# A grouped 1x1 convolution: one extra ring piece of 32 rows, moved by transfers that use 4 of the 16 DMA engines

## The chip, the cores and the metric

The kernel runs on one core of one Trainium2 chip. The metric is the device time of one execution in microseconds (us), and smaller is better. Each profile shows one execution.

The engines are named as the profile names them: PE is the matrix engine (PEld its weight loads), DVE the vector engine, ACT the scalar engine, SP the engine that issues the loads. ACTq and SPq are the queues of ACT and SP, where transfers are issued. Sixteen DMA engines carry the transfers: around 300 us the trace of the kernel before has 16.0 packets under way on average. "Packet" is one record of a transfer in the trace, read here as what one DMA engine moves at a time. A large piece of this kernel makes packets of 24,576 bytes, 128 for its load and 128 for its store. "Instruction fetch" is said here of the packets of 16,384 bytes on queue q8, a queue that the profile lists as "instruction" (12 packets in the kernel before).

## The reference

```python
def reference(x, w):              # x: (1, 512, 512, 192) bf16; w: (1, 1, 4, 48, 48) bf16
    xg = x.reshape(1, 512, 512, 4, 48)
    out = einsum('bhwgc,gcd->bhwgd', xg, w[0, 0])      # cut: the loops over a 1x1 window
    return out.reshape(1, 512, 512, 192)
```

Each of the 262,144 pixels has 192 channels in four groups of 48, and each group is multiplied by its own 48x48 matrix. 100.7 MB come in and 100.7 MB go out.

## The kernel before

Pixels are cut into "pieces". A piece of `size` columns puts `size` consecutive pixels into each of the 128 partitions. One column is thus 128 pixels, and the whole problem is 2048 columns. Loads go into a ring of 256 columns in `x_sb`; results go into a ring of the same size in `o_sb` and are stored from there, piece by piece. The compute engines work in groups of 4 columns: six transposes, a copy by DVE, six matmuls and an eviction from PSUM by ACT (every fourth group is shared with DVE). There are 512 groups.

```python
BIG = 64; RCOLS = 256
HEAD = (4, 4, 8, 16, 32); TAIL = (32, 16, 8, 4, 4)
LOOK = 3; ST_DELAY = 2
# ...
    sizes = list(head) ...                            # head, as many BIG as fit, the rest, tail
    for s in sizes + [BIG] * (mid // BIG) + ([mid % BIG] if mid % BIG else []) + last:
        whole = s == BIG and c % BIG == 0
        pieces.append(Piece(c, s, ("big", c // BIG % (RCOLS // BIG)) if whole else ("own", len(pieces))))
        c += s
# ...
    loads = plan_pieces(cols, HEAD, TAIL)
    stores = plan_pieces(cols, HEAD, TAIL)
    def rows_view(ap, p):                             # 128 rows: 16 landings in the trace
        return ap[128 * p.col:128 * (p.col + p.size), :].rearrange("(p i) c -> p (i c)", p=128)
# ...
        def wait_out_free(wq, g):                     # the ring's place must have been stored
            if g >= body:
                p = store_at[g - body]
                wq.wait(st_sem[p.key], st_val[p])
# ... SP:
            for p in loads:
                wq.wait(t_done, p.g1 - body)          # the ring's place must have been read by PE
                sp.dma_start(ring_view(x_sb, p), rows_view(xf, p)).then_inc(ld_sem[p.key], 16)
# ... ACT:
            def store(p):
                act.dma_start(rows_view(of, p), ring_view(o_sb, p)).then_inc(st_sem[p.key], 16)
            for g in range(NG):
                wait_out_free(wq, g)
                wq.wait(mm_done, g + 1)
                while pending and pending[0][1] <= g:
                    store(pending.pop(0)[0])
                # ... eviction of group g ...
                if g in store_end:                    # a piece is stored once its LAST group is out
                    pending.append((store_end[g], g + ST_DELAY))
```

A wait for a piece is over only when the slowest of the engines that carry it has landed its share: ACT's last wait for the ring, until 424.60 us, is for a store whose fifteenth landing came at 408.76 us and whose last came at 425.07 us (424.58 on the timeline's axis, see below).

Of the kernel before, what the change touches and what calls it, by code (L numbers as in the profile page):

```python
# [11 lines left out]
C = GROUPS * CG  # L12
# [12 lines left out]
BIG = 64  # L25
RCOLS = 256
HEAD = (4, 4, 8, 16, 32)
TAIL = (32, 16, 8, 4, 4)
# [2 lines left out]
LOOK = 3  # L31
ST_DELAY = 2
RING = 8


class Waiter:

    def __init__(self, eng):
        self.eng = eng
        self.seen = {}  # L40
# [7 lines left out]

class Piece:

    def __init__(self, col, size, key):
        self.col, self.size, self.key = col, size, key
        self.g0, self.g1 = col // 4, (col + size) // 4


def plan_pieces(cols, head, tail):
    sizes = list(head) if cols >= sum(head) + sum(tail) else []
    last = list(tail) if sizes else []
    mid = cols - sum(sizes) - sum(last)
    pieces, c = [], 0  # L60
    for s in sizes + [BIG] * (mid // BIG) + ([mid % BIG] if mid % BIG else []) + last:
        whole = s == BIG and c % BIG == 0
        pieces.append(Piece(c, s, ("big", c // BIG % (RCOLS // BIG)) if whole else ("own", len(pieces))))
        c += s
    return pieces


def bass_standalone__grouped__vision_kernel(nc, x, w, out):
    B, H, W_, Cx = x.shape
    assert Cx == C and tuple(w.shape) == (1, 1, GROUPS, CG, CG)  # L70
    npix = B * H * W_

    cols = npix // 128
    assert npix % 512 == 0, "the pixel count must be a multiple of 512"
    NG = cols // 4
    loads = plan_pieces(cols, HEAD, TAIL)
    stores = plan_pieces(cols, HEAD, TAIL)
    load_of = {p.g0: p for p in loads}
    store_at = {g: p for p in stores for g in range(p.g0, p.g1)}
    store_end = {p.g1 - 1: p for p in stores}  # L80
# [1 line left out]
    xf = x.rearrange("b h w c -> (b h w) c")  # L82
    of = out.rearrange("b h w c -> (b h w) c")
    wv = w.rearrange("a b g c d -> c (a b g) d")

    body = RCOLS // 4
    assert body % RING == 0 and BIG % 4 == 0 and RCOLS % BIG == 0
    bigs = [p for p in loads if p.key[0] == "big"]
# [4 lines left out]
    def shared(g):  # L93
        return g % 4 == 1 and g < NG - 3

    dve_prog = [("wcopy", 0)]
    for g in range(NG + LOOK):
        if g < NG:
# [2 lines left out]
        if 0 <= h < NG and shared(h):  # L101
            dve_prog.append(("ev2", h))

    def rows_view(ap, p):
        return ap[128 * p.col:128 * (p.col + p.size), :].rearrange("(p i) c -> p (i c)", p=128)

    def ring_view(t, p):
        at = p.col % RCOLS
        assert at + p.size <= RCOLS
        return t[:, at * C:(at + p.size) * C]  # L110

    with ExitStack() as es:
        block = es.enter_context(nc.Block())
        x_sb = es.enter_context(nc.sbuf_tensor("x_sb", [128, RCOLS * C], BF16))
        o_sb = es.enter_context(nc.sbuf_tensor("o_sb", [128, RCOLS * C], BF16))
# [11 lines left out]
        ld_sem = {k: sem(f"ld_{k[0]}{k[1]}") for k in dict.fromkeys(p.key for p in loads)}  # L127
        st_sem = {k: sem(f"st_{k[0]}{k[1]}") for k in dict.fromkeys(p.key for p in stores)}
        st_val, seen = {}, {}
        for p in stores:  # L130
            seen[p.key] = seen.get(p.key, 0) + 16
            st_val[p] = seen[p.key]
        w_sem, id_sem, e_sem, wb_sem, wc_sem = (sem(s) for s in ("w_sem", "id_sem", "e_sem", "wb_sem", "wc_sem"))
        p0_sem, p1_sem = sem("p0_sem"), sem("p1_sem")
        t_done, mm_done = sem("t_done"), sem("mm_done")
        e1_sem = [sem(f"e1_{i}") for i in range(RING)]
        fa_sem = [sem(f"fa_{i}") for i in range(RING)]
        d2_sem = [sem(f"d2_{i}") for i in range(2)]
# [19 lines left out]
        @block.sync  # L158
        def _(sp):
            wq = Waiter(sp)  # L160
            sp.dma_start(w_sb[:], wv).then_inc(w_sem, 16)  # L161
            for p in loads:
                wq.wait(t_done, p.g1 - body)
                sp.dma_start(ring_view(x_sb, p), rows_view(xf, p)).then_inc(ld_sem[p.key], 16)  # L164

        @block.tensor
        def _(pe):

            def build_weights():
                pe.wait_ge(e_sem, 1)  # L170
                pe.wait_ge(w_sem, 16)
                last = None
                for (tc, r, g, c0_) in WBLOCKS:
                    s0 = ESHIFT - r
                    col = WOFF[tc] + c0_
                    last = pe.matmul(o_ps[:, NOB - 1, col:col + CG], lhsT=esel[:, s0:s0 + 128],  # L176
                                     rhs=w_sb[:, g, :], start=True, stop=True, skip_group_check=True)
                last.then_inc(wb_sem, 1)

            def transposes(g):  # L180
                if g == 0:
                    pe.wait_ge(id_sem, 1)
                p = load_of.get(g)
                if p:
                    pe.wait_ge(ld_sem[p.key], 16)
                ins = []
                for ul in range(2):
                    u = g % body * 2 + ul
                    for tc in range(3):
                        col = u * UC + tc * 128  # L190
                        j = ul * 3 + tc
                        ins.append(pe.transpose(xT_ps[:, g % NXP, j * 128:(j + 1) * 128],  # L192
                                                x_sb[:, col:col + 128], ident[:]))
                if p:
                    ins[1].then_inc(ld_sem[p.key], -16)
                ins[-1].then_inc(t_done, 1)

            def matmuls(g):
                xs = xT_sb[g % NXP]
                waited = [e1_sem[g % RING]]  # L200
                if g == 0:
                    pe.wait_ge(wc_sem, 1)
                if g >= 2:
                    waited.append(fa_sem[(g - 2) % RING])
                    if shared(g - 2):
                        waited.append(d2_sem[(g - 2) // 4 % 2])
                for s in waited:
                    pe.wait_ge(s, 1)
                ins = []
                for ul in range(2):  # L210
                    v = 2 * g + ul
                    for tc in range(3):
                        j = ul * 3 + tc
                        c0_, c1_ = COLR[tc]
                        ins.append(pe.matmul(o_ps[:, v % NOB, c0_:c1_], lhsT=xs[:, j * 128:(j + 1) * 128],  # L215
                                             rhs=wt[:, WOFF[tc]:WOFF[tc] + (c1_ - c0_)],
                                             start=(tc == 0), stop=(tc == 2), skip_group_check=True))
                for i, s in enumerate(waited):
                    ins[1 + i].then_inc(s, -1)
                ins[-1].then_inc(mm_done, 1)  # L220

            def step(g):
                if g + LOOK < NG:
                    transposes(g + LOOK)
                matmuls(g)

            build_weights()
            for g in range(min(LOOK, NG)):
                transposes(g)
            for g in range(loop_g0 if reps else 0):  # L230
                step(g)
            if reps:
                with pe.Fori(0, reps, 1):
                    for g in range(loop_g0, loop_g0 + body):
                        step(g)
            for g in range(loop_g1 if reps else 0, NG):
                step(g)

        @block.vector
        def _(dve):  # L240
            wq = Waiter(dve)
            for (op, g) in dve_prog:
# [4 lines left out]
                if op == "ev1":  # L247
                    wq.wait(t_done, g + 1)
                    dve.tensor_copy(xT_sb[g % NXP][:], xT_ps[:, g % NXP, 0:2 * UC]).then_inc(e1_sem[g % RING], 1)  # L249
                else:  # L250
# [7 lines left out]
        @block.scalar  # L258
        def _(act):
            wq = Waiter(act)  # L260
            pending = []

            def store(p):
                act.dma_start(rows_view(of, p), ring_view(o_sb, p)).then_inc(st_sem[p.key], 16)  # L264

            for g in range(NG):
                wait_out_free(wq, g)
# [3 lines that stand above are left out]
                v = 2 * g  # L271
                u = g % body * 2
                if shared(g):
                    ins = act.copy(o_sb[:, u * UC:(u + 1) * UC], o_ps[:, v % NOB, 0:UC])  # L274
                else:
                    dst = o_sb[:, u * UC:(u + 2) * UC].rearrange("p (u c) -> p u c", u=2)
                    ins = act.copy(dst, o_ps[:, v % NOB:v % NOB + 2, 0:UC])  # L277
                ins.then_inc(fa_sem[g % RING], 1)
                if g in store_end:
                    pending.append((store_end[g], g + ST_DELAY))  # L280
            for (p, _) in pending:
                act.wait_ge(fa_sem[(p.g1 - 1) % RING], 1)
                store(p)
            for p in stores:
                if st_val[p] == seen[p.key]:
                    wq.wait(st_sem[p.key], st_val[p])
# [28 lines left out]
```

## Time and profile before

| | before |
|---|---|
| time, median of 3 runs | 492.08 us (491.52 to 492.30) |
| span of the profiled execution | 489.8 us |
| PE busy | 423.4 us (86%) |
| DMA moved | 201.63 MB, mean 412 GB/s |

From the profile's page of the kernel before: its line of busy times (share of the span, instructions), two lines of its 40 equal slices of the span (DMA is the mean busy share of the 16 DMA engines in tenths, GB/s what they moved), and the two lines of the chain of waits that ended last, by engine and by line.

```profile
PE 423.4 (86%) x6154; PEld 407.9 (83%) x6154; DVE 336.1 (69%) x640; ACT 357.2 (73%) x513; POOL 1.3 (0%) x8
...
DMA  8999999999999999999999999999999999998593
GB/s 297 430 425 423 428 430 433 427 435 425 436 425 432 433 431 433 429 432 431 425 433 430 429 435 429 434 429 433 429 429 426 438 421 434 421 424 351 238 385 149
...
DMA 77%; PE 18%; ACT 1%; another core or an unknown queue 1%; issue 1%; SPq 1%; ACTq 0%
DMA out_dram<-o_sb 73%; PE o_ps L215 10%; PE xT_ps L192 8%; DMA x_sb<-in_x_dram 4%; ACT o_sb L277 1%; SPq L164 0%; ACTq L264 0%; SPq L161 0%; ACTq L46 0%
```

The transfers are the limit: the DMA engines are at 9 tenths in nearly all slices, at about 430 GB/s, and 73% of the chain is stores. But slices 37 to 40 break off. This is the view by stretches for the last 32 us.

```profile
core 0: us, PE busy (x) PEld busy (x) DVE busy (x) ACT busy (x) POOL busy (x), PEclk, DMA share, GB/s
458.00:466.00 8.00, 6.92 (x107) 6.58 (x105) 5.80 (x12) 5.87 (x10) 0.00 (x0) 1.00 0.30 123
466.00:474.00 8.00, 7.32 (x113) 6.95 (x110) 6.36 (x13) 7.33 (x11) 0.00 (x0) 1.00 0.99 416
474.00:482.00 8.00, 3.84 (x30) 3.11 (x30) 0.56 (x1) 2.45 (x4) 0.00 (x0) 0.79 0.64 264
482.00:490.00 8.00, 0.00 (x0) 0.00 (x0) 0.00 (x0) 0.80 (x1) 0.00 (x0) 0.62 0.35 133
```

In two of these stretches the DMA engines are on average only a third busy. An average of 0.30 can be sixteen engines at a third or a few engines at full time. The records of the trace decide: each transfer of 128 rows leaves sixteen landings, read here as one for each engine that carried it. Landings and packet times stand in this document on a clock on which the last landing falls on the end of the span. On the axis of the timelines they are 0.5 us earlier (the last landing of the kernel before is at 489.35 us there). Distances between landings are the same on both; a distance from an instruction to a landing is 0.5 us shorter than the numbers here make it. Of the sixteen landings of one store, the fifteenth and the last are these (us).

```
store of one large piece    15th      last      gap
1st lap of the ring         76.54     76.62     0.1
3rd                        192.98    197.49     4.5
5th                        309.65    318.89     9.2
7th                        424.24    437.96    13.7
final store                485.54    489.84     4.3
```

One engine falls behind by about 2 us a lap. Its store packets take 0.985 to 1.0 us, the others' 0.912. At the end it is the only engine that works: around 463 us and from 486 to 489 us the mean number of busy engines in the trace is 1.0. For the last load PE stands and waits, as the waits of the stretch 440 to 490 us show (engine, line, what it waited for: total us, times, longest us).

```profile
PEld xT_ps L192 <- DMA x_sb<-in_x_dram: 4.1, 1, 4.1
PE xT_ps L192 <- DMA x_sb<-in_x_dram: 3.9, 1, 3.9
```

The timeline of ACT (start in us, duration, instruction, idle time before it and what ended that) gives the last wait for a place in the ring and the last eviction.

```profile
424.60 0.80 ACT L277 CAST o_sb<-o_ps 128x768 bf16<-128x768 f32 x1 [2.76 <-DMA out_dram<-o_sb]
...
482.02 0.80 ACT L277 CAST o_sb<-o_ps 128x768 bf16<-128x768 f32 x1 [0.43 <-PE o_ps L215]
```

The last eviction ends at 482.8 us, fifteen engines have landed everything at 485.5 us, and the span ends with the slow engine at 489.8 us. The last 4.3 us belong to that engine alone.

### The profile page before, as it was taken

How to read it: one execution, taken by the hardware profiler on the slowest of the kernel's cores; microseconds unless marked ns; L12 is line 12 of the kernel's file. 1: busy time of each engine (PE TensorE's matmuls, PEld its weight loads, DVE VectorE, ACT ScalarE, POOL GpSimd, SP SyncE). 2: the span in 40 equal slices, each digit the busy share in tenths (PEclk: the TensorE clock that was granted, in tenths of full speed). 3: DMA queues.
4: the chain of work that ended last, by engine and by line, in shares of the span. 5: the costliest groups of instructions: out<-in, count | busy, mean ns of one | idle time of the engine just before them, and what ended most of it. 6: DMA issues, size and time to landing. Idle time of an engine off the chain costs nothing.

```text
span 489.8 us, 14171 instructions
## 1 busy us (share of the span) xinstructions
PE 423.4 (86%) x6154; PEld 407.9 (83%) x6154; DVE 336.1 (69%) x640; ACT 357.2 (73%) x513; POOL 1.3 (0%) x8
## 2 busy tenths in 40 slices
PE   5999989977997979979798979899798979799962
PEld 5899989977987879878788878898787978799862
DVE  3688878867675767757676757767577757588750
ACT  2788878866785767767677757678586868688862
POOL 1000000000000000000000000000000000000000
PEclk9999999999898998989998989989899989899996
DMA  8999999999999999999999999999999999998593
GB/s 297 430 425 423 428 430 433 427 435 425 436 425 432 433 431 433 429 432 431 425 433 430 429 435 429 434 429 433 429 429 426 438 421 434 421 424 351 238 385 149
DMA packets 11750, 201.63 MB, mean 412 GB/s; under 512 B 1488, under 2 KB 2512, under 8 KB 3536
## 3 DMA queue, kind: packets, MB, share of 16 engines
q1 hardware_dynamic: 5968, 100.68, 48.3%
q10 hardware_dynamic: 5760, 100.67, 48.2%
q8 instruction: 12, 0.20, 0.1%
q14 instruction: 10, 0.08, 0.0%
HBM read 100.68 MB, written 100.66 MB: 411 GB/s over the span
## 4 chain that ended last, share of the span: by engine, by line
DMA 77%; PE 18%; ACT 1%; another core or an unknown queue 1%; issue 1%; SPq 1%; ACTq 0%
DMA out_dram<-o_sb 73%; PE o_ps L215 10%; PE xT_ps L192 8%; DMA x_sb<-in_x_dram 4%; ACT o_sb L277 1%; SPq L164 0%; ACTq L264 0%; SPq L161 0%; ACTq L46 0%
## 5 line engine op out<-in xcount | busy, mean ns | idle before, releaser
L277 ACT CAST o_sb<-o_ps 128x768 bf16<-128x768 f32 x385 | 301.7, 799 | 116.8 <-PE o_ps L215 68.4
L249 DVE COPY xT_sb<-xT_ps 128x768 bf16<-128x768 bf16 x512 | 284.0, 555 | 111.4 <-PE xT_ps L192 104.4
L215 PE MATMUL o_ps<-wt,xT_sb 128*128 128x144 bf16 (+1 forms) x3072 | 308.2, 238 | 47.9 <-ACT o_sb L277 44.8
L192 PE MATMUL xT_ps<-ident,x_sb 128*128 128x128 bf16 x3072 | 265.7, 225 | 7.8 <-DMA x_sb<-in_x_dram 7.3
L215 PEld LDWEIGHTS o_ps<-wt,xT_sb 128*128 128x128 bf16 x3072 | 217.8, 100 | 61.4 <-issue 52.5
L192 PEld LDWEIGHTS xT_ps<-ident,x_sb 128*128 128x128 bf16 x3072 | 205.6, 101 | 9.5 <-DMA x_sb<-in_x_dram 7.6
L255 DVE CAST o_sb<-o_ps 128x384 bf16<-128x384 f32 x127 | 69.8, 550 | 28.0 <-DMA out_dram<-o_sb 26.7
L274 ACT CAST o_sb<-o_ps 128x384 bf16<-128x384 f32 x127 | 61.0, 480 | 8.0 <-PE o_ps L215 5.1
L245 DVE CAST wt<-o_ps 128x480 bf16<-128x480 f32 x1 | 0.7, 658 | 3.2 <-PE o_ps L176 3.2
L176 PE MATMUL o_ps<-w_sb,esel 48*128 48x48 bf16 x10 | 0.6, 210 | 2.6 <-DMA w_sb<-in_w_dram 2.6
L176 PEld LDWEIGHTS o_ps<-w_sb,esel 48*128 48x128 bf16 x10 | 0.5, 112 | 2.5 <-POOL esel L150 2.5
L277 ACT ACT_TABLE_LOAD x1 | 1.3, 1283 | 0.8 <-PEq L300 0.8
L150 POOL TENSOR_SCALAR_AFFINE_SELECT esel<-esel 48x272 bf16<-48x272 bf16 x1 | 0.4, 406 | 0.0
L147 POOL MEMSET esel<- 48x272 bf16 x1 | 0.3, 318 | 0.3 <-POOLq L300 0.3
L154 POOL TENSOR_SCALAR_AFFINE_SELECT ident<-ident 128x128 bf16<-128x128 bf16 x1 | 0.3, 285 | 0.0
L148 POOL MEMSET ident<- 128x128 bf16 x1 | 0.2, 198 | 0.0
L300 POOL MEMSET const-bfloat16-1.0<- 128x1 bf16 x1 | 0.1, 102 | 0.0
L300 POOL MEMSET const-uint8-127<- 128x1 uint8 x1 | 0.1, 102 | 0.0
L300 POOL MEMSET const-float32-0.0<- 128x1 f32 x1 | 0.1, 98 | 0.3 <-issue 0.3
L300 POOL MEMSET const-float32-1.0<- 128x1 f32 x1 | 0.1, 98 | 0.0
## 6 DMA issues: line engine op xcount, KB each, us to landing
x_sb<-in_x_dram SPq DMA_DIRECT2D x30, 3072.0 KB, 25.7
out_dram<-o_sb ACTq DMA_DIRECT2D x30, 3072.0 KB, 45.4
x_sb<-in_x_dram SPq DMA_DIRECT2D x2, 1536.0 KB, 19.7
out_dram<-o_sb ACTq DMA_DIRECT2D x2, 1536.0 KB, 24.9
x_sb<-in_x_dram SPq DMA_DIRECT2D x2, 768.0 KB, 21.5
out_dram<-o_sb ACTq DMA_DIRECT2D x2, 768.0 KB, 20.0
x_sb<-in_x_dram SPq DMA_DIRECT2D x4, 192.0 KB, 27.2
x_sb<-in_x_dram SPq DMA_DIRECT2D x2, 384.0 KB, 24.4
```

The lines of the kernel that those rows point to most:

```text
L147: gp.memset(esel[:], 1.0).then_inc(p0_sem, 1)
L150: gp.affine_select(out=esel[:], in_=esel[:], pattern=[[-1, ECOLS]], compare_op=AluOpType.is_equal, fill=0.0, base=ESHIFT, channel_multipli ...
L154: gp.affine_select(out=ident[:], in_=ident[:], pattern=[[-1, 128]], compare_op=AluOpType.is_equal, fill=0.0, base=0, channel_multiplier=1) ...
L176: last = pe.matmul(o_ps[:, NOB - 1, col:col + CG], lhsT=esel[:, s0:s0 + 128], rhs=w_sb[:, g, :], start=True, stop=True, skip_group_check=True)
L192: ins.append(pe.transpose(xT_ps[:, g % NXP, j * 128:(j + 1) * 128], x_sb[:, col:col + 128], ident[:]))
L215: ins.append(pe.matmul(o_ps[:, v % NOB, c0_:c1_], lhsT=xs[:, j * 128:(j + 1) * 128], rhs=wt[:, WOFF[tc]:WOFF[tc] + (c1_ - c0_)], start=(tc ...
L245: dve.tensor_copy(wt[:], o_ps[:, NOB - 1, 0:WCOLS]).then_inc(wc_sem, 1)
L249: dve.tensor_copy(xT_sb[g % NXP][:], xT_ps[:, g % NXP, 0:2 * UC]).then_inc(e1_sem[g % RING], 1)
L255: dve.tensor_copy(o_sb[:, u * UC:(u + 1) * UC], o_ps[:, v % NOB, 0:UC]).then_inc(d2_sem[g // 4 % 2], 1)
L274: ins = act.copy(o_sb[:, u * UC:(u + 1) * UC], o_ps[:, v % NOB, 0:UC])
L277: ins = act.copy(dst, o_ps[:, v % NOB:v % NOB + 2, 0:UC])
L300: nc = _bacc.Bacc("TRN2", target_bir_lowering=False, num_devices=1)
```

## The change

The intent is to take bytes away from the slow engine. 2048 of the 262,144 pixels go to one extra "narrow" piece of 64 columns that fills only 32 rows of the ring, 0 to 15 and 32 to 47. Its transfers are written with an outer dimension of 4, and 4 engines carry each of them. The other pieces, on all 16 engines, have 16 columns less to carry. In the ring the narrow piece still takes 64 columns, so there are 524 groups instead of 512.

```diff
+FULL = ((0, 128),)
+NARROW = ((0, 16), (32, 16))
+N_NARROW = 1
 ...
-    for s in sizes + [BIG] * (mid // BIG) + ([mid % BIG] if mid % BIG else []) + last:
-        whole = s == BIG and c % BIG == 0
 ...
+    sizes = [(s, FULL) for s in head + [BIG] * (mid // BIG)]
+    sizes += [(BIG, NARROW)] * n_few
+    sizes += [(s, FULL) for s in ([mid % BIG] if mid % BIG else []) + tail]
+    while sizes:
+        s, blocks = sizes.pop(0)
+        room = RCOLS - c % RCOLS          # a piece that would cross the ring's end is cut
 ...
+    def transfers(ap, t, p):
+        for (r0, rows, pix) in p.blocks:
+            px = ap[pix:pix + rows * p.size, :]
+            if p.narrow:
+                view = px.rearrange("(c a i) n -> a c (i n)", a=4, c=rows // 4)
+            else:
+                view = px.rearrange("(p i) n -> p (i n)", p=rows)
+            yield view, t[r0:r0 + rows, at * C:(at + p.size) * C]
 ...
-                sp.dma_start(ring_view(x_sb, p), rows_view(xf, p)).then_inc(ld_sem[p.key], 16)
+                for dram, ring in transfers(xf, x_sb, p):
+                    sp.dma_start(ring, dram).then_inc(ld_sem[p.key], 16)
```

ACT's `store` is changed in the same way as the loads. The planner also lays the end out anew. Before: 30 large pieces, then 32, 16, 8, 4, 4 columns. After: 29 large pieces, the narrow one of 64, a leftover piece of 48, then 16 and 16 (the 32 is cut at the end of the ring), 16, 8, 4, 4.

More of the change, by code (lines that the diff above doesn't have):

```diff
@@ L49, with __init__, plan_pieces @@
 class Piece:
-    def __init__(self, col, size, key):
+    def __init__(self, col, size, key, blocks, pix):
         self.col, self.size, self.key = col, size, key
         self.g0, self.g1 = col // 4, (col + size) // 4
-def plan_pieces(cols, head, tail):
-    sizes = list(head) if cols >= sum(head) + sum(tail) else []
-    last = list(tail) if sizes else []
-    mid = cols - sum(sizes) - sum(last)
-    pieces, c = [], 0
-    for s in sizes + [BIG] * (mid // BIG) + ([mid % BIG] if mid % BIG else []) + last:
-        whole = s == BIG and c % BIG == 0
-        pieces.append(Piece(c, s, ("big", c // BIG % (RCOLS // BIG)) if whole else ("own", len(pieces))))
-        c += s
+        self.blocks = []
+        for (r0, rows) in blocks:
+            self.blocks.append((r0, rows, pix))
+            pix += rows * size
+        self.pix_end = pix
+        self.narrow = len(blocks) > 1
+def plan_pieces(npix):
+    few = BIG * sum(rows for _, rows in NARROW)
+    n_few = N_NARROW if npix >= N_NARROW * few + 128 * (sum(HEAD) + sum(TAIL) + 8 * BIG) else 0
+    cols = (npix - n_few * few) // 128
+    assert cols % 4 == 0
+    head, tail = (list(HEAD), list(TAIL)) if cols >= sum(HEAD) + sum(TAIL) else ([], [])
+    mid = cols - sum(head) - sum(tail)
+    sizes = [(s, FULL) for s in head + [BIG] * (mid // BIG)]
+    sizes += [(BIG, NARROW)] * n_few
+    sizes += [(s, FULL) for s in ([mid % BIG] if mid % BIG else []) + tail]
+    pieces, c, pix = [], 0, 0
+    while sizes:
+        s, blocks = sizes.pop(0)
+        room = RCOLS - c % RCOLS
+        if s > room:
+            sizes.insert(0, (s - room, blocks))
+            s = room
+        whole = s == BIG and c % BIG == 0 and blocks is FULL
+        key = ("big", c // BIG % (RCOLS // BIG)) if whole else ("own", len(pieces))
+        pieces.append(Piece(c, s, key, blocks, pix))
+        c, pix = c + s, pieces[-1].pix_end
+    assert pix == npix
     return pieces
@@ L71, in bass_standalone__grouped__vision_kernel @@
     npix = B * H * W_
-    cols = npix // 128
     assert npix % 512 == 0, "the pixel count must be a multiple of 512"
-    NG = cols // 4
-    loads = plan_pieces(cols, HEAD, TAIL)
-    stores = plan_pieces(cols, HEAD, TAIL)
+    loads = stores = plan_pieces(npix)
+    NG = loads[-1].g1
     load_of = {p.g0: p for p in loads}
@@ L102, in bass_standalone__grouped__vision_kernel @@
             dve_prog.append(("ev2", h))
-    def rows_view(ap, p):
-        return ap[128 * p.col:128 * (p.col + p.size), :].rearrange("(p i) c -> p (i c)", p=128)
-    def ring_view(t, p):
+    def transfers(ap, t, p):
         at = p.col % RCOLS
         assert at + p.size <= RCOLS
-        return t[:, at * C:(at + p.size) * C]
+        for (r0, rows, pix) in p.blocks:
[5 more added lines that the diff above has]
+            yield view, t[r0:r0 + rows, at * C:(at + p.size) * C]
     with ExitStack() as es:
@@ L130, in bass_standalone__grouped__vision_kernel @@
         for p in stores:
-            seen[p.key] = seen.get(p.key, 0) + 16
+            seen[p.key] = seen.get(p.key, 0) + 16 * len(p.blocks)
             st_val[p] = seen[p.key]
@@ L184, in transposes @@
                 if p:
-                    pe.wait_ge(ld_sem[p.key], 16)
+                    pe.wait_ge(ld_sem[p.key], 16 * len(p.blocks))
                 ins = []
@@ L194, in transposes @@
                 if p:
-                    ins[1].then_inc(ld_sem[p.key], -16)
+                    ins[1].then_inc(ld_sem[p.key], -16 * len(p.blocks))
                 ins[-1].then_inc(t_done, 1)
@@ L263, in store @@
             def store(p):
-                act.dma_start(rows_view(of, p), ring_view(o_sb, p)).then_inc(st_sem[p.key], 16)
+                for dram, ring in transfers(of, o_sb, p):
+                    act.dma_start(dram, ring).then_inc(st_sem[p.key], 16)
             for g in range(NG):
```

## The prediction

> **What bounds the kernel now.** Transfers. The table of stretches shows the DMA engines 100% busy from 20 to 440 us at about 430 GB/s while PE is 85 to 93% busy; the chain of waits gives 73% of the span to the stores, as eight links of 45.5 us. But the 16 engines are not equal. Each transfer counts 16 landings in the trace, one per engine. For the store that ends at 76.6 us the last landing comes 0.1 us after the fifteenth; then the gap grows: 4.5 us at 197, 9.2 at 319, 13.7 at 438. One engine lags. Its 24.6 KB store packets take about 0.985 us where the median is 0.912, and it seems also to carry PE's instruction fetches (12 packets, about 0.93 us each). From about 250 us on everything repeats at its pace (60.7 us per ring lap, against 58.2 early on). In slices 37 to 40 the DMA share drops to 0.3 to 0.9: fifteen engines wait, and the laggard is busy back to back until 489.4 us (fifteen engines land the last store at 485.5, the last one at 489.8).
>
> **What the change does.** 2048 of 262144 pixels go to a piece on four engines. [...] No run here shows which engines they are; I assume that the laggard isn't one of them [...].
> - Laggard: 2 packets fewer each way, 2x0.985 + 2x0.912 = 3.8 us less. It is never out of work at the end, so its own finish moves from 489.4 to about 485.7.
> - The four: 8 more packets and 2 fewer, each way: 12x0.912 = +10.9 us. They had a lead of 13.7 us on the laggard, so they finish about level with it. No gain left for more such pieces.
> - Compute: the piece still fills 64 columns of the ring, so 524 groups instead of 512: 12 more transposes, matmuls and evictions. In the last 50 us PE runs at 0.78 us a group without waiting for stores (the last ring wait ends at 424.6 us), so 12x0.78 = +9.4 us there. Before, compute had slack: PE ran to 473.3, then stood 3.9 us for the last load on the laggard. Now without that wait: 476.5 + 9.4 - 0.9 (ring released a little earlier) = 485.0 for the last eviction, +2.6 us to landing = 487.6. One more instruction fetch stall (1.1 us before) is likely.
> - Two extra DMA issues (0.34 to 0.43 us each) and more tail pieces: off the path.
>
> So the DMA gain of 3.8 us is about half eaten by the compute tail: span 489.8 to about 487.9, time **490.1 us** (range 487.3 to 493.5). Faster by over 2%: 0.01; within 2%: 0.93; slower by over 2%: 0.06.
>
> **What would show it.** Right: the narrow transfers move on 4 engines (8 data packets of 24.6 KB on each, each way); gap between fifteenth and last landing unchanged until about 410 us, then smaller; PE's wait for x_sb near 477 us gone; chain of waits ends in PE and ACT, not in a late load; PE busy up by about 9 us; the end of all 16 engines within about 2 us. Wrong: a wait on x_sb of the narrow piece, or four landings behind the rest.
>
> **What would make it wrong.** The laggard among the four: +11 us there, about 501 us. Four engines slower than 0.912 us a packet, or their tail loads late because small load packets alternate with 24.6 KB store packets: up to +3 us. Compute overlapping better, so that the whole 3.8 us shows: 488.

The sum came to 476.5 + 9.4 - 0.9 = 485.0 us for the last eviction, + 2.6 = 487.6 us, put at about 487.9 us of span and 490.1 us of time. That the slow engine is not among the four stands in it as an assumption. What it calls an instruction fetch stall is a stall of PE by "issue" of 1.08 us, until 460.35 us; a fetch ended 0.3 us before it began, but that the fetch caused it is not shown.

## The result, and the profile after

| | before | after |
|---|---|---|
| time, median (range), same rounds | 492.19 us (491.52 to 492.63), 4 runs | 491.18 us (490.61 to 491.86), 4 runs |
| ratio, 95% interval | | 0.9981 (0.9961 to 1.0002) |
| span of the profiled execution | 489.8 us | 490.1 us |
| groups; PE busy | 512; 423.4 us | 524; 430.6 us |

A ratio here and below is the mean time of one kernel's runs over that of the other's of the same rounds, so it is not quite the ratio of the medians that stand beside it. Executions over 1.5% slower than the fastest of the same kernel are left out of the means. The change gained 1.0 us of the forecast 2.0. The time lay inside the predicted range, but the interval of the ratio reaches up to no gain at all. A second measurement later (experiment 12) gave 491.05 against 491.78 us. The profiled execution of the changed kernel is the longest of its four, 491.86 us.

From the page of the changed kernel, the same lines as of before.

```profile
PE 430.6 (88%) x6298; PEld 415.3 (85%) x6298; DVE 344.4 (70%) x655; ACT 365.4 (75%) x525; POOL 1.3 (0%) x8
...
DMA  7999999999999999999999999999999999999557
GB/s 268 432 426 430 427 430 431 433 431 433 428 433 426 437 425 435 427 436 427 435 429 434 429 431 431 432 427 435 429 433 428 431 429 426 424 424 390 218 217 306
...
DMA 77%; PE 18%; ACT 3%; issue 1%; SPq 1%; ACTq 0%
DMA out_dram<-o_sb 73%; PE o_ps L239 10%; PE xT_ps L216 7%; DMA x_sb<-in_x_dram 4%; ACT o_sb L302 3%; SPq L188 0%; ACTq L289 0%; ACT o_sb L299 0%; SPq L184 0%; ACTq L49 0%
```

The chain's shares hardly move, because they are averages over the whole span, and the change acts in its last tenth. ACT's share rises from 1 to 3%. The slices tell more: the last one moves 306 GB/s in place of 149, while slices 38 and 39 are at 218 and 217. The view by stretches shows it better.

```profile
core 0: us, PE busy (x) PEld busy (x) DVE busy (x) ACT busy (x) POOL busy (x), PEclk, DMA share, GB/s
458.00:466.00 8.00, 6.66 (x104) 6.34 (x102) 5.25 (x11) 5.83 (x9) 0.00 (x0) 1.00 0.30 117
466.00:474.00 8.00, 8.00 (x127) 7.80 (x125) 6.80 (x14) 7.05 (x11) 0.00 (x0) 1.00 0.26 104
474.00:482.00 8.00, 7.96 (x122) 7.54 (x120) 6.69 (x13) 7.33 (x11) 0.00 (x0) 1.00 0.99 411
482.00:490.00 8.00, 1.73 (x18) 1.19 (x18) 0.10 (x1) 3.10 (x5) 0.00 (x0) 0.75 0.71 280
```

Before, PE had little left after 474 us (3.84 us of work). Now it works all through the stretch from 474 to 482 us, and the DMA engines are a quarter busy from 466 to 474 us and full from 474 us on. The compute engines have become the ones that finish late, and the transfers have been pushed together behind them. PE's wait for a load is gone in the stretch 440 to 491 us: none of the view's six lines names a DMA. These are three of them ("issue" is time in which the engine waited for nothing that the profile shows):

```profile
PEld o_ps L239 <- issue: 4.2, 5, 1.5
ACT o_sb L299 <- issue: 3.0, 5, 1.8
PE o_ps L239 <- issue: 2.4, 2, 1.3
```

ACT's timeline shows the last wait for the ring, the issue of the store of the leftover piece of 48 columns (the ACTq line), and the last eviction.

```profile
409.13 0.80 ACT L302 CAST o_sb<-o_ps 128x768 bf16<-128x768 f32 x1 [2.78 <-DMA out_dram<-o_sb]
...
473.36 0.34 ACTq L289 DMA_DIRECT2D out_dram<-o_sb  x1
...
485.08 0.80 ACT L302 CAST o_sb<-o_ps 128x768 bf16<-128x768 f32 x1 [0.43 <-PE o_ps L239]
```

From 409.9 us on nothing of the compute waits for a store. It ends at 485.9 us (485.0 was predicted). The landings (us, from the trace's records) say what the DMA engines did.

```
                                before: 15th / last   after: 15th / last
store of a large piece, lap 7   424.24 / 437.96       425.39 / 435.92
last store of a large piece     463.01 / 474.74       465.27 / 473.95
store of the 48-column piece        -                 481.12 / 481.49
final store                     485.54 / 489.84       488.83 / 490.12
```

And the mean number of busy DMA engines at some instants of the last 30 us:

```
before  460.0: 16   462.5: 1   464.0: 1   466.0: 1   467.0 to 477.0: 16   480.0: 1   481.5 to 484.5: 16   486 to 489: 1
after   457.0: 16   462.5: 4   464.5: 5   470.5: 5   473.0: 3   474.0: 0.8   475.0 to 487.5: 16   488.5: 1   489.5: 0.6
```

Before, the slow engine worked on for 4.3 us after the rest. After, the last engine lands 1.3 us after the fifteenth, and the packets say that it is not the slow one. At 480.96 us, with all sixteen engines full, one engine turns from its stores to an instruction fetch of 16 KB (queue q8, 0.92 us). Its packet just before took 1.15 us where the others take 0.69, its packet just after 0.64 us where the others take 0.23. From then on its packets follow one another without a gap, it is the last to land every store from 484.64 us on, and it lands the final store 1.5 us after the fourteenth engine. The slow engine is another one: at 468.7 us, when it and the four of the narrow piece are the only busy engines, a fetch raises the number of busy engines from 5.0 to 6.0.

From 462 to 473 us only three to six engines (the four of the narrow piece and the slow one among them) have work, at 474 us almost none does, and only then does the 48-column store come to all sixteen: it is issued at 473.36 us, when its last group and two more are out. From 475 to 487.5 us all sixteen are full.

### The profile page after: what moved, and what is told of

Read it like the earlier page. It is cut to its first block, busy times and chain, and to the rows that moved or that the text cites. A ratio compares the mean times of both kernels' runs of the same rounds, so it can differ in the third digit from the quotient of the medians.

```text
span 490.1 us, 14506 instructions
## 1 busy us (share of the span) xinstructions
PE 430.6 (88%) x6298; PEld 415.3 (85%) x6298; DVE 344.4 (70%) x655; ACT 365.4 (75%) x525; POOL 1.3 (0%) x8
## 4 chain that ended last, share of the span: by engine, by line
DMA 77%; PE 18%; ACT 3%; issue 1%; SPq 1%; ACTq 0%
DMA out_dram<-o_sb 73%; PE o_ps L239 10%; PE xT_ps L216 7%; DMA x_sb<-in_x_dram 4%; ACT o_sb L302 3%; SPq L188 0%; ACTq L289 0%; ACT o_sb L299 0%; SPq L184 0%; ACTq L49 0%
## 5 line engine op out<-in xcount | busy, mean ns | idle before, releaser
L302 ACT CAST o_sb<-o_ps 128x768 bf16<-128x768 f32 x394 | 308.5, 798 | 106.2 <-PE o_ps L239 60.3
L273 DVE COPY xT_sb<-xT_ps 128x768 bf16<-128x768 bf16 x524 | 291.0, 555 | 108.6 <-PE xT_ps L216 101.2
L239 PE MATMUL o_ps<-wt,xT_sb 128*128 128x144 bf16 (+1 forms) x3144 | 313.6, 237 | 45.9 <-ACT o_sb L302 43.3
L216 PE MATMUL xT_ps<-ident,x_sb 128*128 128x128 bf16 x3144 | 270.8, 224 | 5.6 <-DMA x_sb<-in_x_dram 4.6
L239 PEld LDWEIGHTS o_ps<-wt,xT_sb 128*128 128x128 bf16 x3144 | 221.5, 99 | 59.5 <-issue 50.5
L216 PEld LDWEIGHTS xT_ps<-ident,x_sb 128*128 128x128 bf16 x3144 | 209.6, 101 | 7.1 <-DMA x_sb<-in_x_dram 4.4
L279 DVE CAST o_sb<-o_ps 128x384 bf16<-128x384 f32 x130 | 71.6, 551 | 26.0 <-DMA out_dram<-o_sb 24.5
L299 ACT CAST o_sb<-o_ps 128x384 bf16<-128x384 f32 x130 | 62.4, 480 | 13.5 <-PE o_ps L239 7.6
```

The lines of the kernel that those rows point to most:

```text
L216: ins.append(pe.transpose(xT_ps[:, g % NXP, j * 128:(j + 1) * 128], x_sb[:, col:col + 128], ident[:]))
L239: ins.append(pe.matmul(o_ps[:, v % NOB, c0_:c1_], lhsT=xs[:, j * 128:(j + 1) * 128], rhs=wt[:, WOFF[tc]:WOFF[tc] + (c1_ - c0_)], start=(tc ...
L273: dve.tensor_copy(xT_sb[g % NXP][:], xT_ps[:, g % NXP, 0:2 * UC]).then_inc(e1_sem[g % RING], 1)
L279: dve.tensor_copy(o_sb[:, u * UC:(u + 1) * UC], o_ps[:, v % NOB, 0:UC]).then_inc(d2_sem[g // 4 % 2], 1)
L299: ins = act.copy(o_sb[:, u * UC:(u + 1) * UC], o_ps[:, v % NOB, 0:UC])
L302: ins = act.copy(dst, o_ps[:, v % NOB:v % NOB + 2, 0:UC])
```

## Theories

The first theory, A: two limits stand side by side. One is the slow engine's bytes, which set the end of the kernel before. The other is the compute, whose last part runs without waits; twelve groups more push it back. The change trades one for the other, and the narrow piece would be worth more if its cost were hidden in the middle of the run, or if the last stores were finer (the 48-column piece holds work back that the engines could have done while idle). A rival: the change relieves nothing, since the slow engine's lag is not a matter of its bytes, or the four engines have become slow in their turn. A second rival: the 16 columns and the new cut of the tail loads did the 1 us, and the narrow piece nothing.

## The experiments

All kernels gave correct results. Unless said otherwise an edit is against the changed kernel. Times are medians with their range, and ratios are against the kernel before. The first four kernels ran on one chip in one call, the next four in another, the last four in a third, each with 11 runs of the kernel before (medians 492.21, 491.92 and 491.78 us).

### 1. The narrow piece in the middle (e1_mid4)

```diff
-NARROW = ((0, 16), (32, 16))
+NARROW = ((0, 32),)                                  # one transfer of 32 rows, still 4 engines
 ...
-    sizes += [(BIG, NARROW)] * n_few
+    sizes[len(head) + 15:len(head) + 15] = [(BIG, NARROW)] * n_few
```

> The four-engine piece (32 rows, now rows 0 to 31 in one transfer) stands in the middle, after 15 of the 29 large pieces, not at the end. Theory A (the relief of the slow engine is real, 3.8 us, but at the end the 12 extra groups of compute, 9.4 us, stand in its place): in the middle the groups hide in PE's waits for the stores, so the whole relief shows: about 3.8 us faster than before, 488.4 us (487.3 to 489.5), ratio 0.990 to 0.995. Theory B (the four engines' own extra packets, 10.9 us, give the relief back): place does not matter, about 491.2 us. Theory C (the slow engine is not bound by the bytes that it carries): 492 us.

Measured: 493.05 us (491.26 to 494.32), ratio 1.001 (0.9994 to 1.0025). The expectation of a gain failed. The landings show why. In the middle the engines are only 6 to 7 us ahead of the slow one, not 13.7 (in the kernel before, 6.7 us in the store that ends at 258.19 us). Two laps after the narrow piece, the store of one large piece lands on eleven engines from 282.18 to 286.62 us, on the slow one at 299.74, and on the four at 308.30, 308.38, 310.39 and 311.45 us. The four have overshot and are now the slow ones; they catch up only slowly (one lap later: eleven by 346.69 us, one at 360.57, the four from 366.47 to 369.60). Late small loads cost time at the end as well: in the last 50 us PE waits 9.0 us for loads (experiment 5 takes these waits away). The lead that pays for the narrow piece has to exist before it is spent. Late in the run is the right place for it.

### 2. The extra pixels on fifteen engines (e2_mid15)

```diff
+NARROW = ((0, 120),)                                 # 120 rows: 15 engines
+    sizes[len(head) + 15:len(head) + 15] = [(BIG, NARROW)] * n_few
+            view = px.rearrange("(p i) n -> p (i n)", p=rows)      # also for the narrow piece
```

> The piece has 120 rows and is carried by 15 engines; it stands in the middle. If the slow engine is the sixteenth (the one left out), it has 16 packets of 0.91 to 0.99 us less, 15.2 us, each other engine about one packet more (1.0 us), and there is 1 extra group of compute: theory A then says 479 to 484 us, limited by the other 15 engines and by compute at the end. If the slow engine is one of the first 15, it has one packet more: 492 to 494 us.

"The sixteenth" is the engine that is left out, "the first 15" are those that carry the piece; the trace numbers none of them.

Measured: 502.1 us (498.62 to 506.27), ratio 1.018 (1.0157 to 1.0204; the run of 506.27 us is not in it). Both expectations missed; it lost far more than either said. One part of it was informative: afterwards one engine, the one left out, runs 11 us ahead of all the others (a store's first landing at 251.10 us, the second at 262.28), and another lags (the fifteenth at 271.51, the last at 279.07). So the slow engine is not the one that the fifteen leave out. The view by stretches shows where a part of the time went: 180 to 190 us is an ordinary stretch, from 200 to 220 us the narrow piece is moved.

```profile
core 0: us, PE busy (x) PEld busy (x) DVE busy (x) ACT busy (x) POOL busy (x), PEclk, DMA share, GB/s
180.00:190.00 10.00, 7.34 (x91) 7.12 (x89) 5.13 (x10) 5.52 (x8) 0.00 (x0) 0.83 1.00 430
...
200.00:210.00 10.00, 10.00 (x157) 9.72 (x155) 8.28 (x17) 9.00 (x14) 0.00 (x0) 1.00 1.03 347
210.00:220.00 10.00, 2.86 (x36) 2.69 (x34) 2.04 (x4) 1.99 (x4) 0.00 (x0) 0.74 0.96 366
```

The engines are just as busy, but move 347 and 366 GB/s in place of 430: the load packets of 24.6 KB took 1.30 us on average between 200 and 210 us, where they take 0.91 us otherwise. From these rates, the two stretches lost about 3.4 us of the 10 (an estimate). The rest is not accounted for; at the end PE also waited 8.8 us for small loads, the last of which landed on its slowest engine at 494.92 us. Why these packets were slow is not shown; no run tried fifteen engines with other rows.

### 3. Twelve dead groups, all transfers as before (e3_dead)

The twelve added groups alone: a stretch of 48 columns that nobody loads or stores, but that PE, DVE and ACT process like any other.

```diff
-N_NARROW = 1
+N_NARROW = 0
+DEAD = 48
-    sizes += [(BIG, NARROW)] * n_few
+    sizes += [(DEAD, ())]                            # no blocks: no transfer, no wait
```

> The kernel before with 12 extra groups of compute (48 columns) ahead of the tail, which no transfer fills or empties: the compute part of the change alone. Theory A: the last eviction moves from 482.8 to about 486 us, still inside the time of the slow engine, whose work is unchanged: 492 to 494 us, and in the profile PE works without waiting to the end. If the extra groups all lay on the path: 492.2 + 9.4 = 501 us. If compute never limits the end: 492.2 us and PE has idle gaps at the end.

Measured: 494.13 us (493.06 to 494.54), ratio 1.0037 (1.0024 to 1.0050). The time is 0.1 us above what theory A said, but the trace does not support its reason alone. The ring's end fell elsewhere, so there were six small tail loads in place of five, and PE waited for the last of them. These are the waits of the stretch from 440 to 493 us.

```profile
PEld xT_ps L217 <- DMA x_sb<-in_x_dram: 4.4, 2, 3.7
PE xT_ps L217 <- DMA x_sb<-in_x_dram: 4.0, 2, 3.5
```

A small load is dear on the slow engine. While that engine is alone, its records alternate: one load packet of 1.5 KB (0.065 us), one store packet of 24.6 KB (0.99 us), and so on, so the eight small packets of a load wait for about eight store packets, some 8 us. In the kernel before, the five tail loads land on it at 442.4, 452.2, 461.1, 469.5 and 477.7 us. The experiment mixes two causes; experiments 6 and 11 part them.

### 4. The 48-column store in three (e4_split)

Only the stores change: the leftover piece is loaded as before, and stored in three parts of 16 columns, each once its own groups are out.

```diff
-    loads = stores = plan_pieces(npix)
+    loads = plan_pieces(npix)
+    stores = []
+    for p in loads:
+        stores += [p] if p.size != 48 else [p.part(k) for k in (0, 16, 32)]
 ...
+                view = px.rearrange(...)[:, p.first * C:(p.first + p.size) * C]
```

> The changed kernel, but the store of the 48 columns behind the four-engine piece is cut into three stores of 16, each issued as soon as it is ready (loads unchanged). In the changed kernel all engines ran dry before this store was issued at 473.4 us and were then full until 488 us. Theory A1 (the end is set by compute, last eviction at 485.9 us, plus 2.6 us of landing, and 1.6 us of backlog on the slow engine): the backlog goes, the rest stays: about 1.5 us less than the changed kernel, 489 to 490 us. Theory A2 (the burst of transfers at the end is the limit): 3 us less or more, 488 us or below. If neither matters: 491.2 us.

Measured: 490.12 us (489.20 to 491.27), ratio 0.9958 (0.9944 to 0.9972). This is the fastest kernel, 2.1 us below the kernel before and 1.06 us below the median of the changed kernel. The ratios of the changed kernel (0.9981 and 0.9989) lie outside its interval, though the two kernels' intervals overlap. The view by stretches:

```profile
core 0: us, PE busy (x) PEld busy (x) DVE busy (x) ACT busy (x) POOL busy (x), PEclk, DMA share, GB/s
458.00:466.00 8.00, 6.64 (x102) 6.33 (x101) 5.48 (x11) 5.82 (x9) 0.00 (x0) 1.00 0.32 129
466.00:474.00 8.00, 8.00 (x126) 7.76 (x124) 6.90 (x14) 6.82 (x11) 0.00 (x0) 1.00 0.71 288
474.00:482.00 8.00, 7.61 (x115) 7.08 (x112) 5.95 (x12) 7.18 (x11) 0.00 (x0) 1.00 0.72 292
482.00:490.00 8.00, 1.15 (x12) 0.78 (x12) 0.00 (x0) 2.30 (x3) 0.00 (x0) 0.74 0.51 201
```

The hole between 466 and 474 us is filled (0.71 in place of 0.26), and the last 8 us have less to move (201 in place of 280 GB/s). The last eviction, in ACT's timeline:

```profile
484.16 0.80 ACT L311 CAST o_sb<-o_ps 128x768 bf16<-128x768 f32 x1 [0.43 <-PE o_ps L248]
```

It ends at 484.96 us, fourteen engines have landed at 487.65 us, the fifteenth at 487.70 and the last at 488.15 us. So 3.2 us pass from the last eviction to the end, against 490.12 - 485.88 = 4.2 us in the changed kernel. The fourteen need 2.7 us in both; what became shorter is the lag of the last engine. Between the stores the mean number of busy engines now falls to 4.1 (479 to 480 us) and to 1.9 (482.5 to 483 us), and in such a pause a late engine catches up: the last engine's lag falls from 1.2 us in the store that ends at 484.33 us to 0.6 us in the next. Part of the gain is the eviction, which is 0.9 us earlier; whether the split caused that or the run varied is shown by experiment 12, where the unsplit kernel evicts last at 484.76 us: it varied. The 1.0 us of the shorter tail is the part that can be put down to the split; it rests on one profile of this kernel, and on the times, which fell by as much.

### 5 and 8. The narrow piece earlier, with the tail loaded in few large transfers (e5_mid4_coarse, e8_late4_coarse)

These are experiment 1 again, with the narrow piece after 15 and after 23 large pieces, and without the small tail loads that hurt in it. The tail is loaded in two transfers and stored in parts.

```diff
+TAIL = ()
+PARTS = ((32, 32), (16, 16, 8, 4, 4))                # loads of 64 and 48 columns, stored in these parts
+    sizes[len(head) + 15:len(head) + 15] = [(BIG, NARROW)] * n_few      # e8: 23 in place of 15
```

> The middle version, with the last 112 columns loaded as two transfers (64 and 48) instead of seven; the stores stay fine. In the middle version the last small load reached the slowest engine at 484.7 us, because each transfer gives every engine 8 packets and these alternate one for one with 24.6 KB store packets, so that each small load takes about 8 us there; PE then stood for it. Theory D (the middle version lost its 3.8 us to this late last load): the wait for x_sb at the end is gone and the time falls to 488 to 490.5 us. Theory B (the four engines are the new slow ones and set the end by their bytes): no better than 491.5 us.

> As the middle version with coarse tail loads, but the four-engine piece stands after 23 of the large pieces: the slow engine is some 10 us behind by then, not 6 to 7, and one ring lap is left in which PE still waits for stores, to hide the 12 groups. Theory A with D: 487.5 to 489.5 us, better than the changed kernel and than its version with split stores. If the rows 0 to 31 in one transfer [...] are slower than two blocks of 16, its packets take well over 0.912 us and the time is above 490.5 us.

Measured: 491.13 us (489.43 to 493.86), ratio 0.9984 (0.9960 to 1.0008), for the middle; 490.27 us (490.06 to 491.20), ratio 0.9971 (0.9958 to 0.9984), for the later place. The first fell between the two expectations, the second missed its range by 0.8 us. Against experiment 1 the coarse loads brought about 1.6 us, each kernel taken against the kernel before. In both, the compute was done early, at 481.0 and 479.6 us, 4 to 6 us before the changed kernel's although there are as many groups: added in the middle, they were hidden. Eleven engines were done by 483.7 and 483.2 us, but five engines trailed on: from 484.5 to 490.7 us in the middle version, and from 484.2 to 488.5 us in the later one. With the compute out of the way, five late engines set the end; that they are the slow engine and the four fits their number and their bytes. The later the place, the less they overshoot. No place found did better than experiment 4, though the later one equals it within the ranges.

### 6. The kernel before, tail loaded in one transfer (e6_before_coarse)

```diff
-N_NARROW = 1
+N_NARROW = 0
+TAIL = ()
+PARTS = ((32, 16, 8, 4, 4),)                         # one load of 64 columns, stored in the same parts
```

> The kernel before with only this: its last 64 columns are loaded in one transfer instead of five; no four-engine piece. PE's wait of 3.9 us for the last load goes in any case (the load should land near 445 us instead of 477.7). If the end was set by the bytes of the slow engine (theory A), the time stays at 491.5 to 492.3 us and the gap between the fifteenth and the last landing at the end grows; if it was set by the late last load, 488 to 489.5 us.

Measured: 492.39 us (492.14 to 494.13), ratio 1.0015 (1.0003 to 1.0027). PE's wait of 3.9 us for the last load is gone from the waits after 440 us, and the time has not become shorter (it is 0.1 us above the range of theory A). So that wait was not what held the kernel before back. With the same bytes on the slow engine and PE freed of its wait, the end stayed, and in the profile one engine again lands last by 4.0 us (488.37 and 492.41 us; that this gap would grow did not come true). This is what theory A says: the slow engine's bytes set the end. The rival in which another cut of the tail loads made the gain finds no support here, as this cut gained nothing.

### 7, 9 and 10. More engines in the narrow piece (e7_end8, e9_end7, e10_best7)

If the slow engine were not among those that carry it, a narrow piece of 64 or 56 rows on eight or seven engines would relieve it more (32 or 28 columns less on every engine in place of 16) and would add fewer groups (8 or 9 in place of 12).

```diff
+NARROW = ((0, 32), (32, 32))                         # e7: 8 engines; e9: ((0, 28), (32, 28)), 7 engines
-                view = px.rearrange("(c a i) n -> a c (i n)", a=4, c=rows // 4)
+                view = px.rearrange("(c a i) n -> a c (i n)", a=8, c=rows // 8)    # e9: 7
```

Experiment 10 is experiment 9 with coarse tail loads, `PARTS = ((32, 32), (16, 8, 4, 4, 4))`.

> The changed kernel with 64 rows (0 to 31 and 32 to 63) on eight engines in place of 32 rows on four; the piece stands at the end as in the change. [...] its relief doubles to 7.6 us, eight engines get 7.3 us more each, and there are 8 extra groups of compute instead of 12: compute then ends at about 482.8 us and the time is 487 to 489.5 us. [...] it gets 7.3 us more and the time is 497 to 500 us.

> The changed kernel with 56 rows (0 to 27 and 32 to 59) on seven engines in place of 32 rows on four. [...] it is relieved of 7 packets each way (6.6 us), seven engines get 9 packets more each way than they lose (8.2 us, their lead is 13.7), and there are 9 extra groups of compute (7.0 us) in place of 12: last eviction about 483.6 us, time 488 to 490 us. [...] it carries the piece: 497 to 501 us.

> As the version on seven engines, but the piece stands one large piece earlier, the last columns are loaded as two transfers (64 and 36), and the stores at the end are fine (32, 32, 16, 8, 4, 4, 4). [...] this is the best of all: 486.5 to 489 us, all sixteen engines ending within 2 us of each other. If not, 497 us or more.

In each of the three the first forecast is for a slow engine that is not among those that carry the narrow piece, the second for one that is among them.

Measured: 500.2 us (498.95 to 501.5), ratio 1.0168 (1.0154 to 1.0183), with eight; 502.37 us (502.23 to 503.12), ratio 1.0209 (1.0189 to 1.0228), with seven; 500.86 us (499.92 to 503.2), ratio 1.0176 (1.0157 to 1.0196), with seven and coarse loads. The landings count 18 for the two transfers on eight engines and 16 for those on seven (a transfer on k engines leaves k + 1 landings of its own in these traces when k is below 16), so the numbers of engines are as meant. Each loses about what one expects if the slow engine is among those loaded. With eight, it gets eight packets more and four fewer each way and has no lead to spend, which is 4 x (0.985 + 0.912) = 7.6 us as an estimate from its packet times, against the 8.3 us lost with eight engines (500.2 - 491.92). With seven (eight packets more and 3.5 fewer each way; the nine of the expectation are both ways together) the same sum gives 4.5 x (0.985 + 0.912) = 8.5 us, against 10.6 us lost, and 9.1 us with coarse loads; with the small loads PE also waited 9.3 us for loads at the end. The landings show it directly. In experiment 7 seven engines land the two stores of the narrow piece at 470.7 and by 475.3 us, and one lands them at 482.94 and 486.70 us; in experiment 9 one is alone at 482.48 and 486.52 us, in the changed kernel no engine stands apart like this (all data by 474.36 us). The four of the change do not lose it. This fits a slow engine that is among the eight and among the seven which carried these pieces, and not among the four of the change. Which one it is, no trace names. This also says that the change's 4 was not a small version of something better: a narrow piece on 7 or 8 engines is worse by 9 to 11 us.

### 11. Dead groups with coarse tail loads (e11_dead_coarse)

Experiment 3 without its confusion: the twelve dead groups, no narrow piece, the same bytes on every engine as before, and the tail loaded in two transfers.

```diff
-N_NARROW = 1
+N_NARROW = 0
+DEAD = 48
+TAIL = ()
+PARTS = ((16,), (16, 16, 8, 4, 4))
+    sizes.insert(len(head) + 30, (DEAD, ()))
```

> The kernel before with 12 extra groups of compute and no four-engine piece, as in the run of the dead groups, but the last columns are loaded in two transfers (16 and 48) instead of six, so that no late small load disturbs. Theory A (12 groups cost nothing while the slow engine still sets the end): 491.9 to 493 us, the last eviction near 485 us, no wait for x_sb at the end, and the slow engine's last landing the last event by about 4 us. If the groups by themselves lie on the path: 495 us or more.

Measured: 492.66 us (492.17 to 494.23), ratio 1.0018 (0.9998 to 1.0038). The time is what theory A said. Its detail was not: the slow engine was to be last by about 4 us. In the waits after 440 us no load appears any more:

```profile
PEld o_ps L251 <- issue: 2.7, 4, 1.2
...
PE o_ps L251 <- issue: 1.1, 1, 1.1
```

The last eviction ends at 487.6 us, not 485; in experiment 6, with twelve groups less, it ends at 482.4 us. (The distance is not 12 x 0.78 us, because in experiment 6 the compute was still held by a ring wait at 441.5 us, here last at 424.5 us.) Fifteen engines have landed at 490.31 us and the last one at 490.54 us. The two limits meet: twelve groups, without any relief for the slow engine, bring the compute's end plus 2.7 us level with the slowest engine. This fits that trading one for the other gives so little. Against the changed kernel (491.05 us, experiment 12), which has the same number of groups, it is 1.6 us slower; that is roughly what the relief of the slow engine is worth, as the tails are not cut alike.

### 12. The changed kernel again (e12_after_again)

The changed kernel without any edit, to see how its times and its last eviction vary.

> The changed kernel itself once more, to narrow the interval of its ratio (0.9981, 0.9961 to 1.0002): 491.0 us, ratio 0.997 to 0.999. The profile should again show the last wait for a store ending near 409 us, PE at 0.78 us a group from there, the last eviction near 486 us, few engines busy from 458 to 474 us, and all of them from 475 to 488 us.

Measured: 491.05 us (490.40 to 493.12) in 6 runs, ratio 0.9989 (0.9965 to 1.0012). Its profile is of a faster execution than the first one; the span is 488.9 us. Its last eviction:

```profile
483.96 0.80 ACT L302 CAST o_sb<-o_ps 128x768 bf16<-128x768 f32 x1 [0.43 <-PE o_ps L239]
```

It ends at 484.76 us, and the last engine lands at 488.94 us: again 4.2 us from the one to the other, as in the first profile. The eviction varies by 1.1 us between executions, the 4.2 us do not. Here two engines are late: fourteen have landed at 487.47 us, 2.7 us after the eviction, the other two at 488.78 and 488.94 us. One of the two had carried an instruction fetch at 479.8 us. Not as expected was a short last wait for a store (0.54 us) as late as 423.1 us.

## Why the prediction was right or wrong

- What bounds the kernel: right. Experiment 6 shows that PE's wait is not the limit, and at the end only the slow engine works, so its bytes are the limit that fits.
- The slow engine is not among the four: right. With it among them the prediction put about 501 us, and 491.18 us came; experiments 7 and 9, which fit a slow engine among those loaded, took 500.2 and 502.37 us. It was an assumption: the reason for it is shown by no run here.
- 3.8 us less for the slow engine: the bytes went as forecast, and at the end it no longer stands alone; in the final store it is at most 0.2 us behind the fourteenth engine in the first profile and at most 1.5 us in the second, where it was 4.3 us behind the fifteenth before. How much time this gave it is shown only in part. Its gap at lap 7 is 10.5 us (435.92 - 425.39) in place of 13.7, but at lap 6, before the narrow piece is loaded, it was already 10.9 in place of 12.6. Its own landing is 0.3 us earlier than before at lap 6, 2.0 us at lap 7 and 0.8 us at the last store of a large piece.
- "It is never out of work at the end, so its own finish moves from 489.4 to about 485.7": not so. The final store is not even issued before 485.9 and 484.8 us, so its finish is later than that in any case. In the first profile it was also out of work, but only for 0.4 us (its last small load ends at 474.33, the 48-column store starts at 474.71 us); in the second it was still busy when that store began.
- The four engines finish about level: right in the changed kernel, where the narrow piece comes last, and all sixteen engines land the final store within 1.7 and 1.6 us ("within about 2 us" was forecast). It does not hold when the piece comes earlier, as experiment 1 shows.
- The last eviction at 485.0: right, 485.9 and 484.8 us. One more stall of PE by "issue" of about 1.1 us came too in the first profile (2.4 us in two against 1.1 us in one), not in the second (1.4 us in one).
- "+2.6 us to landing": this step failed. It is about the time from the last eviction to the fifteenth engine's landing in the kernel before, and the sum takes it for the time to the last landing. For fourteen engines it is right: they need 2.7 us before, after, in experiment 12 and in experiment 4. But the last engine needs 4.2 us in both profiles of the changed kernel. One engine in the first profile, two in the second, come to the end with work left over from earlier stores, 1.3 to 1.5 us of it. In the first profile this engine is the one that carried an instruction fetch at 480.96 us. It could not catch up, because from 475 to 487.5 us all sixteen engines were full: the 48-column store, issued only at 473.36 us, had pushed the last transfers together. Experiment 4 shows this part: with that store cut in three there are pauses, the last engine needs 3.2 us, and the time falls to 490.12 us, which is where the prediction had put the changed kernel. The share of the fetch itself is read from the trace; no experiment parts it.
- PE's wait for a load gone: right. The wait for the narrow piece or four landings far behind the rest, named as signs of an error, did not come.
- Who carries the instruction fetches: wrong. In the kernel before, at 464.34 us, a fetch of 16 KB (0.878 us) overlaps in time with packets of the slow engine while that is the only busy one, and the number of busy engines rises from 1.0 to 2.0. So this fetch is on another engine, as is the one at 468.7 us in the changed kernel. The prediction counted only a stall of PE for them, and not that a fetch holds up the stores of the engine that carries it, as the one of 0.92 us at 480.96 us did.

The sum was 485.0 + 2.6 = 487.6 us of span, and it measured 485.9 + 4.2 and 484.8 + 4.2. So the forecast gain of 2.0 us was about halved by one term, 1.6 us too small. The planner's leftover piece had a part in it, which the diff did not show as a cost. Some of the difference between 1.0 and 2.0 us is also the spread of the runs: the interval of the ratio spans from -1.9 to +0.1 us.

Left open: how the 1.5 us divide between the fetch and the crowding, why one engine is slower, which one it is, and why the fifteen-engine layout of experiment 2 moves its packets at 1.30 us.

## What to carry to other kernels

When sixteen parallel engines share the work evenly, look at the landings of one transfer engine by engine: behind an average busy share like the 0.30 from 458 to 466 us here there can be a single late engine, and taking bytes off it is worth at most the distance to the next limit, here the compute (experiment 11: the two tie, 490.31 and 490.54 us). Spend the others' lead only once they have it, so late in the run (here 6 to 7 us in the middle, 13.7 us at the end). And after any change to how the work is cut, look at the size of the last pieces: in this kernel a store is issued once its last group and two more are done, so a leftover of 48 columns next to the end left the transfers idle (busy share 0.26 from 466 to 474 us) and then crowded (0.99 from 474 to 482 us), and cutting it in three was worth as much as the change itself (1.06 and 1.0 us). With all engines full from 475 to 487.5 us, an engine that was held up had no pause to catch up in: it landed the final store 1.5 us after the fourteenth, and it is this engine, not the mean, that ended the kernel.
